# A weight conversion with an empty tick, an earlier second transform, and residual stores from another queue

## The chip, the cores and the metric

The kernel runs on one core of a Trainium2 chip. The metric is the device time of one execution in microseconds (us). The engines are TensorE (PE, with its weight loads as PEld), VectorE (DVE), ScalarE (ACT), GpSimd (POOL) and SyncE (SP), which here only issues DMAs. L624 is line 624 of the kernel before.

## What is computed

Three stages on `x` of 4 x 3136 x 256 (batch, sequence, channels), all in float32: a filter in the frequency domain, then two blocks with a hidden width of 1024.

```python
# stage 1: filter along the sequence
X = np.fft.rfft(x, axis=1)
x = np.fft.irfft(X * (filt_r + 1j * filt_i)[None], n=3136, axis=1)
# stage 2 ("a"): token mixing of rank 32, then w1, relu, w2
u = x + (x.transpose(0, 2, 1) @ U @ V).transpose(0, 2, 1)
x = u + np.maximum(u @ w_ch1, 0.0) @ w_ch2
# stage 3 ("b"): layer norm without offset, times g, then w1b, relu, w2b
xn = (x - mean(x)) / sqrt(var(x) + 1e-6) * g_ln
out = x + np.maximum(xn @ w_ch1b, 0.0) @ w_ch2b
```

## The kernel before

**Numbers.** Every product is made from halves: a matrix is split into a rounded high part and a rest (`ah` and `al`, `hh` and `hl`, `w1h` and `w1l`), and three matmuls stand for one. The weights and the filter's companions arrive as 64-bit words and are converted on the chip.

**The steps.** The 12544 tokens are cut into 25 blocks of up to 512 tokens. Each block has an "a" phase (w1 at L624, w2 at L643 to L645) and a "b" phase (w1b at L624, w2b at L651 to L653). A phase has eight steps, one for each 128 of the hidden width. In a step, `m1` makes one hidden tile: six L624 matmuls into `psh`, relu by ACT into `hh` (L627), the rest by DVE into `hl` (L628). `m2`, two steps behind, multiplies it into `pso`. The phases follow each other as a0 a1 a2 b0 b1 a3 b2 a4 b3 and so on, 400 steps in all. The order of each engine is the order in which the program writes its instructions, and the loop over the steps writes it: first `m1`, then perhaps one tick of the transform, then what `todo` holds for the step, then `m2` and, at a phase's end, `end`, then perhaps a unit, and last a tick or so of the weight conversion.

**Phase ends.** At the end of an "a" phase DVE adds the sums to the input into `x2` (L666), a tile with one buffer, so that L666 of the next "a" phase waits until the last one is stored. Then `todo` spreads over the next steps: adding `al` (L672, names `x`), splitting by ACT and DVE, transposing in place (L675, four and five steps behind), the store of the block to `xd` in DRAM as four DMAs (L702, with the second transpose), its load back in the other layout as `x2t` (L708, at the ninth step, one DMA of 512 KB), and the layer norm's statistics. A "b" phase's end writes the result into `x2t` (L686) and stores it by four DMAs (L694). In the kernel before, all of these stores and loads stand on SP's queue, in program order.

**Units.** A unit makes 448 tokens of the input of stage 2: it loads `ic` (L581) and `wt` (L587, the filtered spectrum from `bd` in DRAM), and for each half of the channels it runs four or more small matmuls and one for the token mixing into `psu` (L595, L597), from which ACT and DVE take `ah` and `al` (L170). `psu` lies in the pool `ps_m`, which has two buffers. Unit 7 is the first of the second batch.

**The transform of batches 1 to 3.** It runs beside the steps, a tick at a time. The generator `rest` yields 36 times for each batch: a load, 15 ticks of the first half, a second load, an empty tick, 17 ticks of the second half (split, product with the filter on POOL at L227, spectrum back through PE, `be` by ACT, then stored to `bd`), and a finish, which makes the units of that batch possible. A credit of RATE a step, from step FFT0 on, decides in which steps a tick runs; once batch 1 is finished the rate is 0.4.

**Weight conversion.** 18 jobs turn the 64-bit words into halves. A job's pieces are: absolute value and low word by ACT, four integer operations by DVE (`words`, L746 to L749), a product and a sum by POOL (L763, L764, into `ct`), then `keep` and `last`. For w1 and w2, `keep` is ACT's copy into the high part and `last` POOL's or DVE's subtraction (L842). For w1b, `keep` is DVE's product with g (`wg`, L832), and behind every second job a `center` takes off the column means: two matmuls with a matrix of 1/256 into `psw` (L848, again in pool `ps_m`), DVE's subtraction (L852), ACT's copies and POOL's rests (L854). Each tick moves every live job on by one piece. `brisk` is set once the first units are made; from then on there is one tick a step, for steps 0 to 23 or so. POOL also issues the loads of these weights, with a DMA of its own queue for each job (L740, `stg`).

The lines of the loop that set where a tick of the transform stands:

```python
if idx > FFT0:
    credit += RATE if 1 not in tstk else 0.4
    if credit >= 1:
        credit -= 1
        next(rest, None)
```

Of the kernel before, what the change touches and what calls it, by code (L numbers as in the profile page):

```python
# [20 lines left out]
P = 128  # L21
# [22 lines left out]
PARTS, UPARTS = (0, 1, 2, 5, 6, 8), 10  # L44
CALLS = (0, 0, 0, 1) + tuple(range(1, 24))
LEAD = 3
FFT0, RATE = 26, 0.75

XTURN, XREAD, XSTAT, XROOT = (3, 4), 8, (10, 11), 12
BW = 32  # L50
# [88 lines left out]
def fft_mixer_kernel(ctx: ExitStack, tc: tile.TileContext, x, U, V, flt, w1, w2, gln, w1b, w2b,  # L139
                     c_fwd32, c_d32, c_e32, c_fwd, c_inv, c_e, c_d, c_w, out):  # L140
    nc = tc.nc
# [43 lines left out]
    xd = [dram.tile([BLK, D], F32, name=f"xd{k}") for k in range(NBLK)]  # L185
# [388 lines left out]
    def blen(k):  # L574
        return min(BLK, NTOK - k * BLK)
# [79 lines left out]
    def end(ph):  # L655
# [3 lines left out]
        if kind == "a":  # L659
            x2 = mp.tile([P, BLK // BW, BW, KT], F32, tag="x2", name="x2", bufs=1)  # L660

            def cut(t, dh):
                return t[k][:, dh, :n].rearrange("p (j c) -> p j c", c=BW)

            for dh in range(KT):
                nc.vector.tensor_tensor(out=x2[:, :n // BW, :, dh], in0=acc[dh][:, :n].rearrange("p (j c) -> p j c", c=BW),  # L666
                                        in1=f32(cut(acth, dh)), op=ALU.add)
            while len(todo) <= XROOT:
                todo.append([])
            for dh in range(KT):  # L670
                o, ah, al = x2[:, :n // BW, :, dh], cut(acth, dh), cut(actl, dh)
                todo[dh].append(lambda o=o, al=al: nc.vector.tensor_tensor(out=o, in0=o, in1=f32(al), op=ALU.add))  # L672
                todo[dh + 1].append(lambda o=o, ah=ah: acopy(ah, o))
                todo[dh + 2].append(lambda o=o, ah=ah, al=al: sub(al, o, f32(ah)))
                todo[XTURN[dh]].append(lambda o=o: nc.vector.transpose(out=o, in_=o))  # L675
            todo[XTURN[-1]].append(lambda: x2store(k, x2))
            todo[XREAD].append(lambda: x2load(k))
            for j, at in enumerate(XSTAT):
                todo[at].append(lambda j=j: x2stat(k, j))
            todo[XROOT].append(lambda: x2root(k))  # L680
            return
# [16 lines left out]
    def x2store(k, x2):  # L698

        n = blen(k)  # L700
        for i in range(P // BW):
            nc.sync.dma_start(xd[k].rearrange("(j t) (i c) -> t j i c", t=BW, i=P // BW)[:, :n // BW, i],  # L702
                              x2[i * BW:(i + 1) * BW, :n // BW].rearrange("p j c k -> p j (c k)"))

    def x2load(k):
# [37 lines left out]
    def words(s, h, t):  # L743

        hb, tb = h.bitcast(I32), t.bitcast(I32)
        nc.vector.tensor_scalar(out=h, in0=h, scalar1=TOP, scalar2=None, op0=ALU.min)  # L746
        nc.vector.tensor_scalar(out=tb, in0=hb, scalar1=3, scalar2=None, op0=ALU.logical_shift_left)
        nc.vector.scalar_tensor_tensor(out=tb, in0=s[:, :, 1], scalar=-0x80000000, in1=tb, op0=ALU.bitwise_and, op1=ALU.bitwise_or)
        nc.vector.tensor_scalar(out=hb, in0=tb, scalar1=-0x800000, scalar2=None, op0=ALU.bitwise_and)  # L749

    def to32(i, s, keep, last):


        p, n = s.shape[:2]
        tags = ("xs", "ya") if brisk and i % 2 else ("yh", "yl")
        h, lf = (fp.tile([P, 512], F32, tag=tag, name=f"c{tag}", bufs=3 if tag == "ya" else 2)[:p, :n] for tag in tags)
        nc.scalar.activation(out=h, in_=s[:, :, 1].bitcast(F32), func=AF.Abs, scale=2.0 ** -112)
        nc.scalar.activation(out=lf, in_=s[:, :, 0].bitcast(U32), func=AF.Copy, scale=2.0 ** -52)
        yield
        t = fp.tile([P, 2 * (D + R)], F32, tag=("fhi", "flo")[i % 2], name="ct", bufs=2)[:p, :n]  # L760
        words(s, h, t)
        yield
        nc.gpsimd.tensor_tensor(out=lf, in0=lf, in1=h, op=ALU.mult)  # L763
        nc.gpsimd.tensor_tensor(out=t, in0=t, in1=lf, op=ALU.add)  # L764
        yield
        keep(t)
        yield
        last(t)
        yield

    after = []
    aside, brisk = nc.vector, False

    def stagger(jobs):

        words, live, fetched = {}, [], 0
        after.clear()

        def fetch(n):
            nonlocal fetched  # L780
            while fetched < min(n, len(jobs)):
                words[fetched] = jobs[fetched][0]()
                fetched += 1

        def advance():
            nonlocal live
            while after:
                after.pop()()
            live = [g for g in live if next(g, 0) is None]

        for n in range(4):
            fetch(n + 1)
            yield
        for i in range(len(jobs) + 4):
            if brisk:
                advance()
            if i < len(jobs):
                live.append(to32(i, words.pop(i), *jobs[i][1:]))
                next(live[-1])
            yield  # L800
            advance()
            if brisk:
                fetch(i + 3)
            yield
            if not brisk:
                advance()
                fetch(i + 3)
                yield
# [73 lines left out]
    with tc.manual_schedule():  # L882
# [6 lines left out]
        def chain():  # L889
            for b in range(1, NB):  # L890
                yield from fft(b)

        first = First()
        pr = stagger([w_job("w1", w1, 0, "wt"), w_job("w1", w1, 1, "wt"), v_job(0), v_job(1)] + [w_job(nm, w, j) for nm, w, j in (
            ("w2", w2, 0), ("w1", w1, 2), ("w1", w1, 3), ("w2", w2, 1), ("w2", w2, 2),
            ("w2", w2, 3), ("w1b", w1b, 0), ("w1b", w1b, 1), ("w2b", w2b, 0), ("w1b", w1b, 2), ("w1b", w1b, 3),
# [64 lines left out]
        brisk = True  # L961
# [61 lines left out]
```

## Time and profile before

| | |
|---|---|
| median of 3 runs | 1402.79 us |
| the runs | 1405.51, 1402.31, 1402.79 us |
| the profiled execution's own time | 1402.46 us |
| its span in the trace | 1400.7 us |
| PE busy | 1358.4 us, 97% |
| DVE busy | 802.0 us, 57% |
| ACT busy | 549.8 us, 39% |
| POOL busy | 173.9 us, 12% |
| moved by DMA | 152.29 MB, mean 109 GB/s |

The page of the profile gives for each engine how long it was busy. An engine close to the whole span sets the time; for such an engine the few microseconds in which it stood still are read one by one: when they were, and which instruction of which engine ended them. The granted clock (PEclk) says how fast PE was allowed to run in a stretch, as a share of full speed. Busy time at half clock is longer, so it is not idle time and doesn't show as such. Times in the timelines count from the start of the span.

### The profile page before, as it was taken

How to read it: one execution, taken by the hardware profiler on the slowest of the kernel's cores; microseconds unless marked ns; L12 is line 12 of the kernel's file. 1: busy time of each engine (PE TensorE's matmuls, PEld its weight loads, DVE VectorE, ACT ScalarE, POOL GpSimd, SP SyncE). 2: the span in 40 equal slices, each digit the busy share in tenths (PEclk: the TensorE clock that was granted, in tenths of full speed). 3: DMA queues.
4: the chain of work that ended last, by engine and by line, in shares of the span. 5: the costliest groups of instructions: out<-in, count | busy, mean ns of one | idle time of the engine just before them, and what ended most of it. 6: DMA issues, size and time to landing. Idle time of an engine off the chain costs nothing.

```text
span 1400.7 us, 20122 instructions
## 1 busy us (share of the span) xinstructions
PE 1358.4 (97%) x7678; PEld 1173.4 (84%) x7678; DVE 802.0 (57%) x1533; ACT 549.8 (39%) x1048; POOL 173.9 (12%) x170
## 2 busy tenths in 40 slices
PE   8888899999899999999999999999999999999998
PEld 8576789887788888888888887888888888888898
DVE  4777974478554455667554445766444444444444
ACT  4864434366433334445333334544322222222222
POOL 3737511022100001111000001111000000000000
PEclk9899999999999999999999999999999999999999
DMA  9735237555526424444345344353122013201111
GB/s 282 246 77 162 75 82 196 166 163 166 158 56 159 125 89 129 120 142 130 74 118 152 91 131 131 98 168 84 58 65 65 16 49 84 65 16 31 46 46 38
DMA packets 140576, 152.29 MB, mean 109 GB/s; under 512 B 61472, under 2 KB 117696, under 8 KB 140384
## 3 DMA queue, kind: packets, MB, share of 16 engines
q1 hardware_dynamic: 131840, 132.37, 33.4%
q0 software_dynamic: 7776, 17.44, 5.1%
q8 instruction: 60, 0.98, 0.3%
q10 hardware_dynamic: 864, 1.20, 0.2%
q14 instruction: 36, 0.29, 0.1%
HBM read 103.44 MB, written 47.54 MB: 108 GB/s over the span
## 4 chain that ended last, share of the span: by engine, by line
PE 82%; DVE 4%; ACT 2%; DMA 1%; issue 1%; SPq 0%; POOL 0%; DVEq 0%; ACTq 0%; POOLq 0%
PE psh L624 36%; PE pso L653 6%; PE pso L652 6%; PE pso L651 6%; PE pso L643 6%; PE pso L644 5%; PE pso L645 5%; PE psu L595 3%; PE ps L199 2%; PE ps L201 2%; PE ps L200 2%; DVE ya L234 1%; PE psu L597 1%; ACT xs L167 1%; PE pt L255 1%
## 5 line engine op out<-in xcount | busy, mean ns | idle before, releaser
L628 DVE SCALAR_TENSOR_TENSOR hl<-psh,hh 128x512 fp32r<-128x512 f32 (+1 forms) x400 | 271.0, 679 | 427.1 <-ACT hh L627 426.7
L627 ACT ACTIVATE hh<-psh 128x512 fp32r<-128x512 f32 (+1 forms) x400 | 234.9, 588 | 604.5 <-PE psh L624 603.8
L624 PE MATMUL psh<-ah,wb 128*128 128x512 f32 (+1 forms) x800 | 276.7, 387 | 0.2 <-DVE hl L628 0.2
L651 PE MATMUL pso<-wb,hh 128*128 128x256 f32 x784 | 221.1, 282 | 1.1 <-DVE x L666 1.1
L653 PE MATMUL pso<-wb,hl 128*128 128x256 f32 x784 | 221.8, 283 | 0.0
L652 PE MATMUL pso<-wb,hh 128*128 128x256 f32 x784 | 221.7, 283 | 0.0
L624 PEld LDWEIGHTS psh<-ah,wb 128*128 128x128 f32 x800 | 150.3, 189 | 28.0 <-DVE hl L628 0.8
L624 PE MATMUL psh<-ah,w1h 128*128 128x512 f32 (+1 forms) x400 | 157.6, 394 | 5.4 <-DVE hl L628 5.4
L643 PE MATMUL pso<-hh,w2h 128*128 128x512 f32 (+1 forms) x400 | 155.0, 388 | 6.8 <-DVE x2t L686 3.5
L651 PEld LDWEIGHTS pso<-wb,hh 128*128 128x128 f32 x784 | 149.7, 191 | 7.5 <-DVE x L666 1.3
L624 PE MATMUL psh<-al,w1h 128*128 128x512 f32 (+1 forms) x400 | 155.8, 390 | 0.0
L624 PE MATMUL psh<-al,wb 128*128 128x512 f32 (+1 forms) x400 | 155.5, 389 | 0.0
L624 PE MATMUL psh<-ah,w1l 128*128 128x512 f32 (+1 forms) x400 | 155.1, 388 | 0.0
L644 PE MATMUL pso<-hl,w2h 128*128 128x512 f32 (+1 forms) x400 | 154.5, 386 | 0.0
L652 PEld LDWEIGHTS pso<-wb,hh 128*128 128x128 f32 x784 | 149.7, 191 | 5.5
L645 PE MATMUL pso<-hh,w2l 128*128 128x512 f32 (+1 forms) x400 | 154.2, 386 | 0.0
L653 PEld LDWEIGHTS pso<-wb,hl 128*128 128x128 f32 x784 | 149.8, 191 | 0.0
L227 POOL TENSOR_TENSOR xs<-xs,ft 128x512 f32<-128x512 f32 x42 | 55.1, 1312 | 391.4 <-ACT xs L167 383.8
L643 PEld LDWEIGHTS pso<-hh,w2h 128*128 128x128 f32 x400 | 75.4, 188 | 22.5 <-DVE x2t L686 4.4
L624 PEld LDWEIGHTS psh<-ah,w1h 128*128 128x128 f32 x400 | 75.9, 190 | 20.0 <-DVE hl L628 7.5
L624 PEld LDWEIGHTS psh<-ah,w1l 128*128 128x128 f32 x400 | 75.6, 189 | 16.0
L645 PEld LDWEIGHTS pso<-hh,w2l 128*128 128x128 f32 x400 | 75.2, 188 | 15.4
(170 smaller groups left out, 1932.2 us busy)
## 6 DMA issues: line engine op xcount, KB each, us to landing
ft<-flt SPq DMA_DIRECT2D x42, 512.0 KB, 4.4
xd<-x SPq DMA_DIRECT2D x96, 128.0 KB, 2.8
x2t<-xd SPq DMA_DIRECT2D x24, 512.0 KB, 4.5
wt<-bd SPq DMA_DIRECT2D x24, 448.0 KB, 5.8
out<-x2t SPq DMA_DIRECT2D x84, 128.0 KB, 2.1
xt<-x SPq DMA_DIRECT2D x42, 224.0 KB, 3.7
zd<-ze SPq DMA_DIRECT2D x42, 224.0 KB, 2.8
zt<-zd SPq DMA_DIRECT2D x42, 224.0 KB, 3.2
```

The lines of the kernel that those rows point to most:

```text
L199: nc.tensor.matmul(o, lh, rh, start=True, stop=False)
L227: (cross or nc.gpsimd).tensor_tensor(out=xs, in0=xs, in1=ft[:, :, 1], op=ALU.mult)
L595: nc.tensor.matmul(ps[:, m:UN:UW], t[:, m, dh * P:(dh + 1) * P], ic[:, m, :], start=m == 0, stop=False, skip_group_check=True)
L624: nc.tensor.matmul(ps[:, :n], w[:, kt, fs], a[:, kt, :n], start=j == 0, stop=j == 3 * KT - 1)
L627: nc.scalar.activation(out=hh[:, :n], in_=ps[:, :n], func=AF.Relu)
L628: nc.vector.scalar_tensor_tensor(out=hl[:, :n], in0=ps[:, :n], scalar=0.0, in1=f32(hh[:, :n]), op0=ALU.max, op1=ALU.subtract)
L643: nc.tensor.matmul(o, wh[:, f, ds], hh[:, :n], start=f == 0, stop=False)
L644: nc.tensor.matmul(o, wh[:, f, ds], hl[:, :n], start=False, stop=False)
L645: nc.tensor.matmul(o, wl[:, f, ds], hh[:, :n], start=False, stop=f == FT - 1)
L651: nc.tensor.matmul(o, hh[:, cs], wh[:, f, :], start=f == 0 and c % 2 == 0, stop=False, skip_group_check=True)
L652: nc.tensor.matmul(o, hh[:, cs], wl[:, f, :], start=False, stop=False, skip_group_check=True)
L653: nc.tensor.matmul(o, hl[:, cs], wh[:, f, :], start=False, stop=f == FT - 1, skip_group_check=True)
```

## The change

Three things are changed. A job of the weight conversion passes an empty tick between POOL's sum and `keep`, so that the engine that takes the sum does so one step later than before; the jobs' loop is one tick longer. FFT0 and RATE become 22 and 0.72 (26 and 0.75 before). The four stores of a residual block (L702) are issued by POOL and no longer by SP. By the two added lines, line numbers from L765 on are two higher in the changed kernel (L832 is L834 there, L842 is L844, L848 is L850, L852 is L854, L854 is L856).

```diff
-FFT0, RATE = 26, 0.75
+FFT0, RATE = 22, 0.72
...
         for i in range(P // BW):
-            nc.sync.dma_start(xd[k].rearrange("(j t) (i c) -> t j i c", t=BW, i=P // BW)[:, :n // BW, i],
+            nc.gpsimd.dma_start(xd[k].rearrange("(j t) (i c) -> t j i c", t=BW, i=P // BW)[:, :n // BW, i],
                               x2[i * BW:(i + 1) * BW, :n // BW].rearrange("p j c k -> p j (c k)"))
...
         nc.gpsimd.tensor_tensor(out=t, in0=t, in1=lf, op=ALU.add)
         yield
+        if brisk:
+            yield
         keep(t)
         yield
         last(t)
...
-        for i in range(len(jobs) + 4):
+        for i in range(len(jobs) + 5):
```

What this does to the engines' order shows at three places. On PE, the first center (`psw`, behind two jobs of w1b) and the unit that follows it in the kernel before, with the names as above:

```order
L645 MATMUL pso<-hh,w2l 128x512
L848 MATMUL psw<-wg,ones 128x512 x2
L624 MATMUL psh<-ah,w1h 128x512
L624 MATMUL psh<-al,w1h 128x512
L624 MATMUL psh<-ah,w1l 128x512
```

and the same place in the changed kernel, from the end of a step on:

```order
L645 MATMUL pso<-hh,w2l 128x512
L595 MATMUL psu<-ic,wt 112x128 x4
L597 MATMUL psu<-v_sb,tk 128x448
L595 MATMUL psu<-ic,wt 112x128 x4
L597 MATMUL psu<-v_sb,tk 128x448
L850 MATMUL psw<-wg,ones 128x512 x2
L624 MATMUL psh<-ah,w1h 128x512
```

Before, the center stands between two steps, and the unit stands one whole step (six L624 rows and the six of w2) further on; now the center stands directly behind the unit.

On DVE, the integer operations of a job (L746 to L749, with the names `cxs`, `cyh`) around the first two products with g (`wg`), before:

```order
L566 COPY wt_1270<-psw 112x512
L832 TENSOR_SCALAR wg<-ct,g_sb 128x512
L746 TENSOR_SCALAR cxs<-cxs 128x512
L747 TENSOR_SCALAR ct<-cxs 128x512
L748 SCALAR_TENSOR_TENSOR ct<-stg,ct 128x512
L749 TENSOR_SCALAR cxs<-ct 128x512
L628 SCALAR_TENSOR_TENSOR hl<-psh,hh 128x512 x2
L832 TENSOR_SCALAR wg<-ct,g_sb 128x512
```

and in the changed kernel:

```order
L566 COPY wt_1269<-psw 112x512
L746 TENSOR_SCALAR cxs<-cxs 128x512
L747 TENSOR_SCALAR ct<-cxs 128x512
L748 SCALAR_TENSOR_TENSOR ct<-stg,ct 128x512
L749 TENSOR_SCALAR cxs<-ct 128x512
L628 SCALAR_TENSOR_TENSOR hl<-psh,hh 128x512
L834 TENSOR_SCALAR wg<-ct,g_sb 128x512
L628 SCALAR_TENSOR_TENSOR hl<-psh,hh 128x512
```

The product with g has moved behind the integer operations of the next job and behind one `hl`.

On SP, at the end of the "b" phase ahead of the second batch's first unit (`out` is the result's store, `x2t` the load of a residual block, `ic` and `wt` a unit's loads), before:

```order
L694 DMA out<-x2t_3093 32x4x256 x4
L708 DMA x2t_3814<-xd4_97 128x4x256
L581 DMA ic_3836<-c_inv 112x448
L587 DMA wt_3835<-bd1_119 112x1024
L581 DMA ic_3862<-c_inv 112x448
L587 DMA wt_3861<-bd1_119 112x1024
```

and in the changed kernel:

```order
L694 DMA out<-x2t_3127 32x4x256 x4
L581 DMA ic_3815<-c_inv 112x448
L587 DMA wt_3814<-bd1_119 112x1024
L286 DMA xt_3818<-x 112x512
L286 DMA xt_3820<-x 112x512
L708 DMA x2t_3824<-xd4_97 128x4x256
L581 DMA ic_3868<-c_inv 112x448
```

The first unit's two loads now stand ahead of the load of the residual block, and the first two loads of the next batch's transform (`xt`) between them.

## Rows read from the trace of the kernel before

**Rows 1.** Page, busy time: engine, us, share of span, instructions.

```profile
PE 1358.4 (97%) x7678; PEld 1173.4 (84%) x7678; DVE 802.0 (57%) x1533; ACT 549.8 (39%) x1048; POOL 173.9 (12%) x170
```

**Rows 2.** Stretches: length, PE PEld DVE ACT POOL busy, PEclk, DMA share, GB/s.

```profile
125.00:157.00 32.00, 27.88 (x118) 21.60 (x118) 25.69 (x41) 14.00 (x26) 20.54 (x19) 0.95 0.40 120
157.00:184.00 27.00, 24.91 (x105) 19.25 (x104) 25.32 (x41) 12.58 (x20) 14.98 (x13) 1.00 0.36 93
184.00:296.00 112.00, 112.00 (x686) 100.05 (x685) 62.76 (x128) 46.10 (x88) 9.33 (x15) 1.00 0.56 152
...
376.00:388.00 12.00, 7.53 (x36) 6.50 (x35) 2.74 (x5) 2.64 (x6) 0.00 (x0) 0.86 0.90 242
...
384.60:388.00 3.40, 3.40 (x17) 3.31 (x17) 0.62 (x1) 0.54 (x1) 0.00 (x0) 0.50 0.93 225
```

**Rows 3.** Waits of PE, 98 to 184 us: us in sum, times, longest.

```profile
PE psh L624 <- DVE hl L628: 4.6, 5, 2.0
PE pso L643 <- DVE x L666: 3.2, 2, 1.7
```

**Rows 4.** Timeline of DVE: start, us, instruction, in brackets idle before and releaser.

```profile
133.55 0.49 DVE L832 TENSOR_SCALAR wg<-ct,g_sb 128x512 f32<-128x512 f32 x1 [2.19 <-POOL ct L764]
...
134.41 0.55 DVE L747 TENSOR_SCALAR ct<-cyh 128x512 int32<-128x512 int32 x1
```

**Rows 5.** Timeline of PE in the conversions: behind the unit, and two waits.

```profile
144.88 0.40 PE L624 MATMUL psh<-ah,w1h 128*128 128x512 f32 x1
...
152.53 0.80 PE L624 MATMUL psh<-ah,w1h 128*128 128x512 f32 x1 [2.01 <-DVE hl L628]
...
170.79 0.50 PE L643 MATMUL pso<-hh,w2h 128*128 128x512 f32 x1 [1.71 <-DVE x L666]
```

**Rows 6.** Timeline of DVE from the first block's transpose to the second's `x`.

```profile
158.73 0.70 DVE L675 STREAM_TRANSPOSE x<-x 128x512 f32<-128x512 f32 x1
...
164.30 1.28 DVE L852 TENSOR_TENSOR wg<-wg,psw 128x512 f32<-128x512 f32 x2 [1.24 <-PE psw L848]
...
165.96 1.40 DVE L747 TENSOR_SCALAR ct<-cyh 128x512 int32<-128x512 int32 x1
...
170.05 1.28 DVE L666 TENSOR_TENSOR x<-pso,ah 128x512 f32<-128x512 f32 x2
```

**Rows 7.** Timeline of DVE, the unit's subtraction behind the first center.

```profile
149.04 0.69 DVE L170 TENSOR_TENSOR al<-psu,ah 128x256 fp32r<-128x256 f32 x2 [0.45 <-ACT ah L167]
```

**Rows 8.** Timelines of SP's queue and of PE, unit 7.

```profile
376.61 0.54 SPq L708 DMA_DIRECT2D x2t<-xd  x1
...
377.83 0.38 SPq L587 DMA_DIRECT2D wt<-bd  x1
...
384.12 1.17 PE L595 MATMUL psu<-ic,wt 112*128 112x112 f32 x6 [4.47 <-DMA wt<-bd]
```

**Rows 9.** Line 587 from 370 to 390 us, two loads.

```profile
DMA to landing us min/median/max: 6.2/7.0/7.7
```

**Rows 10.** Waits of PE, 285 to 376 us, and one row of its timeline.

```profile
PE ps L199 <- ACT be L167: 3.3, 8, 1.0
...
600.61 0.36 PE L595 MATMUL psu<-ic,wt 112*128 112x112 f32 x1 [0.96 <-ACT be L167]
```

**Rows 11.** Line 702 from 150 to 200 us, eight stores.

```profile
DMA to landing us min/median/max: 2.2/2.8/3.0
```

**Rows 12.** POOL's DMA issues: timeline (one) and groups by line (busy, mean ns).

```profile
134.15 0.56 POOL L957 DMA_DIRECT2D d_sb<-c_d  x1
...
L740 POOL DMA_DIRECT2D stg<-w2b x4 | 3.0, 762 | 11.8 <-issue 6.1 <-ACT hh L627 2.6 <-ACT wt L167 2.3
...
L740 POOL DMA_DIRECT2D stg<-w1b x4 | 2.3, 574 | 7.3 <-DVE cxs L749 2.6 <-ACT ah L167 1.6 <-ACT w2h L167 1.6
```

**Rows 13.** Timeline of DVE, second block's transpose to third block's `x`.

```profile
187.23 0.71 DVE L675 STREAM_TRANSPOSE x<-x 128x512 f32<-128x512 f32 x1
...
192.55 0.69 DVE L666 TENSOR_TENSOR x<-pso,ah 128x512 f32<-128x512 f32 x1 [0.72 <-DMA xd<-x]
```

## The prediction

> **What bounds the kernel now.** I read the page first. TensorE (PE) is busy 1358.4 us of a span of 1400.7 us, 97% [rows 1]. The change removes no matmul, so all it can win is PE's idle time, about 42 us in the whole run, and the stretches in which PE ran at a lower clock. Next I cut the span into stretches [rows 2]. In the last two thirds of the weight conversions (125 to 184 us) PE is idle for 32.00 − 27.88 = 4.12 us and 27.00 − 24.91 = 2.09 us, and the granted clock is 0.95 in the first of these two; from 184 to 296 us PE is never idle; the twelve microseconds around the second batch's first unit have 4.5 us of idle time at a clock of 0.86. DVE is the busy neighbour in the conversions: 25.69 us of 32 and 25.32 us of 27, so a wait that goes there meets an engine with almost no room.
>
> Then the waits. Between 98 and 184 us PE waits for DVE, five times for `hl` (4.6 us) and twice for the residual `x` (3.2 us) [rows 3]. I read DVE's own order to see what makes it late [rows 4]: twice it waits for POOL's sum `ct` before it can write `wg` (2.19 us at 133.55 us; the row at 127.69 us is of the same kind, with 2.09 us), and the second such wait stands some 3 us ahead of the first block's `x`. So the first edit aims at a place where PE does lose time.
>
> **The empty tick.** Before, the piece whose sum POOL was given in one tick is taken by ACT or DVE in the next; now one tick later. Removed from DVE: 2.09 + 2.19 us of waits for POOL. The center of `w1b`'s second half moves a step, so DVE's 1.24 us wait for `psw` and the 1.28 us of work behind it [rows 6] stand after `x` at 170.05 us and no longer ahead of it; PE's 1.71 us wait at that place [rows 5] should shrink. Added: the first center's two matmuls now stand behind the unit and not 2.7 us ahead of it. They take a buffer of the unit's own pool, which DVE's `al` of the unit's first half must free. DVE is behind there: it ends that subtraction (its second piece, the first of two from 149.04 us) at about 149.4 us [rows 7], while PE came out of the unit at 144.88 us [rows 5]. So PE waits up to 4.5 us, and 0.2 us if DVE keeps all of the 4.28 us won ahead of it; I take the middle, 2.4 us. Behind the waiting `psw` stands the next step's whole L624 row. Behind each center, `hl` waits for `hh`, which on ACT stands behind two copies of the centered weights and two absolute values. PE's 2.01 us wait at 152.53 us [rows 5], right behind the first center, is of this kind, and the change leaves its cause. PE's waits before 125 us stay as they are, since nothing on DVE waits for POOL in steps 3 to 6. So of the 4.12 + 2.09 = 6.2 us idle, 2.0 us stay and 2.4 us come new: 1.8 us gained, less half of a slow stretch (0.8 us, half of the 1.7 us priced below) that a wait of 2.4 us may bring: −1.0 us. The bounds: everything goes, with the clock, which at 0.95 over 32 us cost 1.6 us, 7.8 us; I use 6.5 us, since one wait of the new kind must stay. On the other side 4.5 us are added at the center and next to nothing goes: +4. Nearest row for my value: DVE's busy 25.3 to 25.7 us per stretch, which the tick does not lower.
>
> **The transform from step 22 on.** The first tick moves from step 28 to 24, the last from 74 to 73. The first unit of batch 1 stays behind step 75. What changes is SP's order. Before, its `wt` load stood behind the 512 KB load of `x2t` and was issued at 377.83 us, landing 6.2 us later at 384.03 us; PE had been ready at 384.12 − 4.47 = 379.65 us [rows 8, 9]. Now `ic` and `wt` stand right behind the four stores of `out`, so `wt` goes out one issue earlier, at 377.83 − 0.6 = 377.2 us, without the 512 KB ahead of it; at the 242 GB/s of that stretch [rows 2] these took 2.2 us. Landing: 377.2 + 6.2 − 2.2 = 381.2 us, wait 1.6 us in place of 4.47: −2.9 us. The clock: from 384.6 to 388 us PE ran at 0.50 [rows 2], which cost 1.7 us. A wait of 2.01 us was followed by such a stretch (152.53 us, clock 0.95 over the 32 us), one of 1.71 us was not (170.79 us, clock 1.00) [rows 2, 5]; so at 1.6 us I count it as gone: −1.7 us. Sum −4.6 us; bounds −0.6 us (only the earlier issue counts) and −6.2 us (all of it).
>
> The ticks of the second half spread a little: 22 steps before, 23 now. Its eight waits of PE for ACT's `be` sum to 3.3 us [rows 10]; scaled by 0.72/0.75 and with fewer runs of three in a row, about −0.7 us. But a unit's turn at step 59 now meets such a tick, and where a unit met one in the later trace PE waited 0.96 us (600.61 us) [rows 10]. Together +0.3 us. Batches 2 and 3 keep their grid of 0.4 a step, one tick further along: their stalls stay.
>
> **The stores on POOL's queue.** Each residual block is stored by four DMAs of 32 x 16 pieces of 256 bytes. From SP they land at most 3.0 us after their issue [rows 11]. No POOL-issued DMA of 512 pieces is in the trace. POOL takes 574 ns to issue one of 128 pieces (`w1b`) and 762 ns for one of 256 (`w2b`) [rows 12]; the line through both gives 574 + 3 × 188 = 1138 ns for 512, an estimate. Bounds: 574 ns, the cheaper row (no price per piece), and 2 × 762 = 1524 ns. So four take 2.3 to 6.1 us, by the line 4.6 us, and 7.6 us until the last has landed.
>
> Who waits for that? `x2` has one buffer, so the next block's `x` (L666) waits for the store. In steady state 11 steps of some 2.8 us (170.05 to 192.55 us is eight steps) lie between, and the load L708 stands four steps behind: both hidden. But a0, a1 and a2 follow each other, and there it is three steps, 8.2 us. For a0 the store can begin when the transpose ends, 158.73 + 0.70 = 159.4 us; `x` stood at 170.05 us [rows 6], and at 170.05 − 1.24 − 1.28 = 167.5 us once it is ahead of the center: 8.1 us against 7.6. I take 0. For a1: 187.23 + 0.71 = 187.94 us, `x` at 192.55 us after a wait of 0.72 us for this very store, 4.6 us in all [rows 13]. With 5.3 to 9.1 us in place of 4.6, `x` comes 0.7 to 4.5 us later, by the line 3.0 us. PE was never idle there [rows 2], so it has some slack; half is my value, +1.5 us, bounds 0 and +4. On POOL itself the fetch of `w2b`'s last piece is queued behind a0's stores: 4.6 us later, covered by two steps' room. The store of block 3 stands ahead of L227's filter product of the transform, which ACT and then PE wait for behind it: one more wait of the eight's mean, 3.3 / 8 = 0.4 us. SP loses 96 issues, but no wait of PE is for an SP issue behind a store, so that gains nothing.
>
> What speaks for a dearer store is a rule, weighed here by itself. The trace has a POOL-issued DMA beside DVE's L747: 0.56 us at 134.15 us [rows 4, 12], no longer than the 574 ns of the `w1b` fetches. The Trainium skill, "SBUF — State Buffer", section "SBUF: two separate sides", holds that DVE in a two-port mode locks POOL out of writing descriptors, and that such a DMA of some 620 ns took some 3100 ns; by that the store of a0 and a1 would be far dearer, and the third rival below would be the likeliest. The row does not bear it out for one DMA of few pieces; no run here shows it for 512.
>
> **Sum.** −1.0 − 4.6 + 0.3 + 1.5 + 0.4 = −3.4 us against the profiled execution's 1402.46 us (span 1400.7 us and 1.8 us around it): 1399.06 us. The median, 1402.79 us, is 0.33 us above that execution, so 1399.4 us.
>
> **Rivals.** First: the tick does all that it can, −6.5 us in place of −1.0, and the store of a1 hides: 1399.4 − 5.5 − 1.5 = 1392.4 us. For it: DVE's two waits and the center's were 5.5 us in sum, ahead of PE's waits. Against it: DVE's load and the center behind the unit. Second: the `wt` load doesn't do what I say, since the DMA queues are busy with `out` and `xt` anyway and PE's wait stays over 2 us with its slow clock: 1399.4 + 4.0 = 1403.4 us. For it: the DMA share of 0.90 in that stretch [rows 2]. Third, slower: a store costs POOL 1.8 us or more. Then a0's four take 7.2 + 3.0 = 10.2 us against 8.1, PE waits 2.1 us, and a1's `x` is 5.6 us late, some 4 us on PE; both waits are over 2 us and each brings a slow stretch of 1.7 us: +9.5 us in place of my +1.5, 1407.4 us and up. For it: DVE and POOL stretch each other, L747 took 1.40 us beside POOL's subtraction at 165.96 us [rows 6] and 0.55 us beside its DMA at 134.41 us [rows 4]. Against it: POOL's DMA rows vary little.
>
> **How the numbers follow.** The measurement can tell a change from none at about 0.3%, 4.2 us: faster is below 1398.6, slower above 1407.0 us. My forecast has 0.53; its time is just inside "same", so 0.24 of that lies below 1398.6 and 0.29 within; first rival 0.20, all faster; second 0.15, all same; third 0.12, all slower. Faster 0.44, same 0.44, slower 0.12. The range must reach into the first rival and to the foot of the third: 1391.5 to 1407.0 us.
>
> **What would show it.** In the changed trace: DVE's waits for POOL's `ct` at L834 gone; a PE wait at `psw` behind the unit of the first center; PE's wait for `wt` near 385 us below 2 us and no clock of 0.50 behind it; four L702 rows on POOL near 1.1 us each; `x` at step 25 some 3 us later with a wait for the store. Wrong it would be if the stores cost over 1.8 us each, if PE's idle time between the conversions' second third and their end fell below 2.5 us or rose above 10, or if `wt` still landed after 383 us.

## The result and the profile after

The changed kernel takes 1414.8 us, the median of four runs (1412.2 to 1416.12), against 1402.81 us before: a ratio of 1.0079, 95% interval 1.0059 to 1.0100. It is slower by 11 us (8 to 14), where 1399.4 us and a range from 1391.5 to 1407.0 us had been forecast. The profiled execution of the changed kernel is its fastest one, 1412.2 us with a span of 1410.4 us, 9.7 us longer than the span before; what the traces show below adds up to those 9.7 us.

Where they are shows if the start of each of the 400 steps (its first L624 matmul) is compared between the two traces. The offset after minus before, in us, at the beginning of some steps:

| step | 0 | 10 | 14 | 22 | 49 | 75 | 76 | 399 |
|---|---|---|---|---|---|---|---|---|
| after − before | 0.6 | 0.7 | 4.2 | 7.4 | 7.5 | 11.5 | 10.7 | 9.4 |

Steps 10 to 22 (the conversions) lose 6.8 us, the second half of the transform (49 to 75) loses 4.0 us, the first unit of the second batch (75 to 76) wins 0.8 us, and the rest wins 1.3 us. The head of the program, ahead of step 0, is the same code in all kernels of this study and lasts from 98.1 to 101.5 us in their profiled executions, shortest in the kernel before. So the traces are compared from step to step, and the times by their medians.

The stretches of the changed kernel, columns as in [rows 2]:

```profile
125.00:157.00 32.00, 27.93 (x117) 21.20 (x116) 24.92 (x35) 13.90 (x26) 20.70 (x18) 0.89 0.42 123
157.00:184.00 27.00, 22.02 (x88) 15.75 (x86) 23.78 (x34) 9.60 (x17) 15.41 (x15) 1.00 0.41 103
...
394.80:398.20 3.40, 3.40 (x16) 3.36 (x17) 0.49 (x1) 0.54 (x1) 0.00 (x0) 0.52 1.08 275
```

Against [rows 2]: the idle time of the first is the same, 4.1 us, but its granted clock fell from 0.95 to 0.89; the second has 5.0 us of idle time where there were 2.1. The third is the first unit of the second batch, which still runs at half the clock.

The waits of PE in the changed kernel from 98 to 190 us (us in sum, times, longest), to be held against [rows 3]:

```profile
PE psh L624 <- DVE hl L628: 7.0, 6, 2.2
PE psw L850 <- DVE al L170: 3.2, 1, 3.2
PE psu L595 <- ACT wt L167: 1.0, 1, 1.0
PE pso L643 <- DVE x L666: 0.9, 1, 0.9
PE pso L645 <- POOL w2l L844: 0.6, 1, 0.6
```

The wait for `x` shrank from 3.2 to 0.9 us, as the empty tick meant it to. The waits for `hl` grew from 4.6 to 7.0 us, and a new one stands at `psw`, the center behind the unit. By steps: gone are the 2.0 us at step 14 (for `hl`) and the 1.7 us at step 18 (for `x`); new are 3.2 us at step 11 (`psw`) and 0.8, 1.2, 1.6 and 2.2 us at steps 15, 16, 20 and 21 (`hl`).

DVE's own waits in the same stretch, first before, then after:

```profile
DVE wg L832 <- POOL ct L764: 4.3, 2, 2.2
...
DVE hl L628 <- ACT hh L627: 2.9, 4, 1.1
DVE wg L852 <- PE psw L848: 1.2, 1, 1.2
```

```profile
DVE hl L628 <- ACT hh L627: 9.0, 6, 2.8
...
DVE wg L854 <- PE psw L850: 2.8, 1, 2.8
```

This is the heart of the result. DVE's 4.3 us of waiting for POOL are gone. In their place it waits 6.1 us longer for ACT's `hh` and 1.6 us longer for PE's `psw`. Why ACT is late shows in its timeline behind the first center of the changed kernel:

```profile
151.02 1.23 ACT L167 ACTIVATE wb<-wg 128x512 fp32r<-128x512 f32 x2 [3.98 <-DVE wg L854]
152.15 0.62 ACT L167 ACTIVATE wb<-ct 128x512 fp32r<-128x512 f32 x1
152.67 0.65 ACT L757 ACTIVATE cyh<-stg 128x512 f32<-128x512 f32 x1
153.23 0.65 ACT L758 ACTIVATE cyl<-stg 128x512 f32<-128x512 uint32 x1
153.78 0.58 ACT L627 ACTIVATE hh<-psh 128x512 fp32r<-128x512 f32 x1
```

The two copies of the centered weights wait for DVE; behind them stand the next job's copy and the absolute values of the job after it, and only then `hh`. Before the change the center lay in a step that had the copies but no absolute values. The same stands behind the second center, with the same 2.8 us.

The two absolute values are 1.1 of these 2.8 us. The rest shows because DVE has nothing left to do there. In the kernel before it had the next job's four integer operations between the center's subtractions and `hl`, and `hl` did not wait (behind the second center, L852 at 164.30 us in [rows 6]):

```profile
165.51 0.42 DVE L746 TENSOR_SCALAR cyh<-cyh 128x512 f32<-128x512 f32 x1
...
169.45 0.68 DVE L628 SCALAR_TENSOR_TENSOR hl<-psh,hh 128x512 fp32r<-128x512 f32 x1
```

In the changed kernel DVE stands idle there, and the integer operations follow one step later, behind a job's last subtraction (L844; L746 starts at 157.73 us):

```profile
150.30 1.28 DVE L854 TENSOR_TENSOR wg<-wg,psw 128x512 f32<-128x512 f32 x2 [2.80 <-PE psw L850]
154.39 0.69 DVE L628 SCALAR_TENSOR_TENSOR hl<-psh,hh 128x512 fp32r<-128x512 f32 x1 [2.81 <-ACT hh L627]
...
156.01 1.79 DVE L844 TENSOR_TENSOR wb<-ct,wb 128x512 fp32r<-128x512 f32 x1
```

And the center itself, on PE:

```profile
146.51 3.75 PE L850 MATMUL psw<-wg,ones 128*128 128x512 f32 x4 [3.17 <-DVE al L170]
...
150.48 0.63 PE L624 MATMUL psh<-al,w1h 128*128 128x512 f32 x1
```

The 3.17 us are the wait for a buffer of the unit's pool. L624, 0.39 us otherwise, takes 0.63 us behind it: from 148 to 158 us the granted clock is 0.77 in the changed kernel.

### The profile page after: what moved, and what is told of

The parts are those of the page before. It is cut to its first block, busy times and chain, and to the rows that moved or that the text cites. A ratio compares the mean times of both kernels' runs of the same rounds, so it can differ in the third digit from the quotient of the medians.

```text
span 1410.4 us, 20171 instructions
## 1 busy us (share of the span) xinstructions
PE 1358.9 (96%) x7678; PEld 1170.9 (83%) x7678; DVE 810.0 (57%) x1533; ACT 549.5 (39%) x1048; POOL 239.2 (17%) x270
## 4 chain that ended last, share of the span: by engine, by line
PE 84%; DVE 8%; ACT 3%; DMA 2%; issue 2%; POOL 1%; SPq 0%; DVEq 0%; ACTq 0%; POOLq 0%
PE psh L624 35%; PE pso L653 6%; PE pso L651 6%; PE pso L652 6%; PE pso L643 5%; PE pso L644 5%; PE pso L645 5%; PE psu L595 3%; PE ps L199 2%; PE ps L200 2%; PE ps L201 2%; DVE hl L628 1%; PE pz L423 1%; ACT xs L167 1%; DVE ya L234 1%
## 5 line engine op out<-in xcount | busy, mean ns | idle before, releaser
L624 PE MATMUL psh<-ah,wb 128*128 128x512 f32 (+1 forms) x800 | 276.7, 387 | 0.5 <-DVE hl L628 0.5
L624 PEld LDWEIGHTS psh<-ah,wb 128*128 128x128 f32 x800 | 150.3, 189 | 28.0 <-DVE hl L628 0.7
L624 PE MATMUL psh<-ah,w1h 128*128 128x512 f32 (+1 forms) x400 | 158.2, 395 | 8.0 <-DVE hl L628 7.9
L624 PE MATMUL psh<-al,w1h 128*128 128x512 f32 (+1 forms) x400 | 155.7, 389 | 0.0
L624 PE MATMUL psh<-al,wb 128*128 128x512 f32 (+1 forms) x400 | 155.5, 389 | 0.0
L624 PE MATMUL psh<-ah,w1l 128*128 128x512 f32 (+1 forms) x400 | 154.8, 387 | 0.0
L702 POOL DMA_DIRECT2D xd<-x x100 | 64.6, 654 | 520.6 <-DVE x L675 519.9
L624 PEld LDWEIGHTS psh<-ah,w1h 128*128 128x128 f32 x400 | 75.8, 189 | 24.2 <-DVE hl L628 11.6
L624 PEld LDWEIGHTS psh<-ah,w1l 128*128 128x128 f32 x400 | 75.5, 189 | 15.9
```

What stands on the lines that cost most here:

```text
L624: nc.tensor.matmul(ps[:, :n], w[:, kt, fs], a[:, kt, :n], start=j == 0, stop=j == 3 * KT - 1)
L702: nc.gpsimd.dma_start(xd[k].rearrange("(j t) (i c) -> t j i c", t=BW, i=P // BW)[:, :n // BW, i], x2[i * BW:(i + 1) * BW, :n // BW].rearra ...
```

## The experiments

All times below are medians; "before" was run beside each and had 1403.2 to 1403.7 us there. Differences to before are worked out from the ratio, times 1403 us. T is the empty tick, F the transform's new start and rate, Q the stores on POOL's queue.

### The three parts, each alone

**t_only** adds only the two edits of the tick to the kernel before:

```diff
+        if brisk:
+            yield
...
-        for i in range(len(jobs) + 4):
+        for i in range(len(jobs) + 5):
```

> Only the empty tick is added to the kernel before. Theory A (the first center now stands behind the unit, waits there for DVE to free its PSUM buffer, and a stretch of lower clock follows): most of the loss is here, 1402.8 + 6 to 8 = 1409 to 1411 us, with PE waiting about 3 us at the first psw (L850) and a granted clock near 0.77 in the ten microseconds behind it. Rival B (the stores on POOL's queue hold up POOL's sums and the centered weights): the tick alone costs nothing or gains 1 us, 1401.5 to 1403 us, and the wait at psw is below 1 us.

Measured: 1408.78 us against 1403.58, ratio 1.0044 (1.0029 to 1.0059), some 6.2 us slower, just below theory A's band. Its two signs are there: a wait of 3.19 us at the first `psw`, and a granted clock of 0.75 from 148 to 158 us. PE's waits from 98 to 190 us sum to 12.5 us, where they were 8.5.

**f_only** changes one line of the kernel before:

```diff
-FFT0, RATE = 26, 0.75
+FFT0, RATE = 22, 0.72
```

> Only FFT0 and RATE are changed. Theory A: the second half of the second transform loses about 4 us by its new neighbours (a wait for x2t, one for yh, a unit beside a tick), the first unit's load gains about 1 us: 1405 to 1407 us. Rival B (the transform is not at fault, those waits come from POOL's filter product behind the stores): 1398 to 1402 us, with PE's waits in that half at 3.5 us or less.

Measured: 1410.34 us, ratio 1.0053 (1.0034 to 1.0073), 7.4 us slower; more than theory A said. The waits of PE from 98 to 400 us hold what was known from the changed kernel and one more:

```profile
PE psu L595 <- DMA wt<-bd: 3.3, 1, 3.3
PE pso L651 <- DVE x L666: 2.4, 1, 2.4
PE ps L199 <- ACT be L167: 2.2, 6, 0.7
PE pso L643 <- DVE x2t L686: 1.5, 1, 1.5
PE psu L595 <- ACT be L167: 1.0, 1, 1.0
PE ps L199 <- ACT yh L167: 0.9, 1, 0.9
```

The 2.4 us are at step 26. SP's queue and the timelines of ACT and DVE tell why:

```profile
188.24 2.17 SPq L702 DMA_DIRECT2D xd<-x  x4
190.46 1.82 SPq L286 DMA_DIRECT2D xt<-x  x3
...
194.53 0.63 ACT L167 ACTIVATE hi<-xt 112x512 fp32r<-112x512 f32 x1 [3.11 <-DMA xt<-x]
...
195.19 0.69 DVE L170 TENSOR_TENSOR lo<-xt,hi 112x512 fp32r<-112x512 f32 x1 [3.05 <-ACT hi L167]
195.80 1.28 DVE L666 TENSOR_TENSOR x<-pso,ah 128x512 f32<-128x512 f32 x2
```

The transform's first loads `xt` stand on SP behind the second block's stores, which wait for DVE's transpose. They land late, ACT waits for them, DVE waits for ACT, and `x` (L666) of the third block stands behind that on DVE. A granted clock of 0.55 from 196.5 to 200 us follows, so that steps 22 to 27 lose 3.0 us.

**q_only** changes the queue of the stores alone:

```diff
-            nc.sync.dma_start(xd[k].rearrange("(j t) (i c) -> t j i c", t=BW, i=P // BW)[:, :n // BW, i],
+            nc.gpsimd.dma_start(xd[k].rearrange("(j t) (i c) -> t j i c", t=BW, i=P // BW)[:, :n // BW, i],
```

> Only the four stores of a residual block are issued by POOL. Theory A: near nothing, 1402.5 to 1405 us, the stores at 0.65 us each on POOL. Rival B: 5 us or more, 1408 us and up, with PE's idle time from 157 to 376 us grown by 4 us.

Measured: 1405.89 us, ratio 1.0022 (1.0011 to 1.0033), 3.1 us slower. The time lies 0.9 us above theory A's band and 2.1 us below rival B's. The line of the stores, from 150 to 220 us:

```profile
L702 POOL DMA_DIRECT2D xd<-x x12: 651/652/762, 163.0 to 215.7; - x12
...
DMA to landing us min/median/max: 2.7/3.1/4.5
```

A store of 512 pieces costs POOL 0.65 us, and lands up to 4.5 us after its issue (3.1 us in the median), where SP's landed within 3.0 us (2.8 us) [rows 11]. `x` at step 26 now waits 2.0 us for the store on DVE (0.72 us before, [rows 13]), and PE 0.7 us for `x`.

**fq** has F and Q without T.

> The transform from step 22 at 0.72 and the stores on POOL, without the empty tick. Theory A (part of the early transform's loss is that on SP's queue its first loads xt stand behind the second block's stores, which wait for DVE's transpose, so DVE waits for xt ahead of x at step 26): with the stores on POOL that wait goes, the two parts cost less than their sum, 1402.8 + 7.4 + 3.1 - 4 = 1409 us. Rival (the parts add up): 1413 us.

Measured: 1408.27 us, ratio 1.0030 (1.0019 to 1.0042), 4.2 us slower, as theory A said, and no slower than F alone. In its trace no wait of PE is left at step 26: with the stores on POOL the loads `xt` have no store ahead of them on SP, and go out from 166.5 us on, not 190.5 us as in f_only. So F and Q share a loss: steps 22 to 27 lose 3.0 us in f_only, 1.0 us in q_only, nothing in fq and 0.1 us in the changed kernel. This is a part of why the three parts alone (6.2 + 7.4 + 3.1 = 16.7 us) sum to more than the whole change (11 us); the rest is not located, and the intervals are wide (F alone: 4.8 to 10.2 us).

### Why the tick costs

**after_psw** puts the center's sums into another pool, in the changed kernel, and **t_psw** does the same with T alone:

```diff
-            ps = ps_m.tile([P, 512], F32, tag="m", name="psw")
+            ps = ps_t.tile([P, 512], F32, tag="t", name="psw")
```

> The changed kernel with one line changed: the center's sums (psw) lie in PSUM's one-buffer pool ps_t in place of the unit's pool ps_m, so that they wait for no buffer that DVE must free. Theory A: PE's wait of 3.2 us at the first psw goes, with the lower clock behind it: 5 to 6 us less than the changed kernel, about 1409 us. Rival (DVE is late anyway and the wait comes back at the next hl): within 1.5 us of the changed kernel, 1413 to 1416 us, a wait of 2 us or more at L624 in its place.

> Only the empty tick, with the center's sums in the one-buffer PSUM pool ps_t. Theory A (the tick's loss is the center's wait behind the unit and the low clock after it): the 3.2 us wait goes and the time comes 4 us below the tick alone, 1404 to 1406 us. Rival (the tick moves the load of DVE and ACT onto worse steps, and the center is only where it shows): within 1.5 us of the tick alone, 1407 to 1410 us.

Measured: 1411.01 us for after_psw, ratio to before 1.0063 (1.0046 to 1.0079), by the ratios 2.2 us and by the medians 3.8 us below the changed kernel; 1407.32 us for t_psw, ratio 1.0029 (1.0019 to 1.0039), 2.1 us and 1.5 us below the tick alone. after_psw lies between its two expectations, t_psw in the band of its rival. The waits of after_psw from 98 to 190 us, and one stretch of it:

```profile
PE psh L624 <- DVE hl L628: 10.3, 8, 2.2
```

```profile
125.00:157.00 32.00, 27.12 (x124) 20.96 (x122) 27.62 (x40) 14.77 (x27) 20.98 (x18) 1.00 0.43 123
```

The wait at `psw` is gone and the same three microseconds come back at `hl`, as the rival had it: 12.8 us of waits in sum, 12.7 in the changed kernel. What is won is the clock, 1.00 in place of 0.89 over 32 us: steps 10 to 22 lose 3.9 us in place of 6.8 (t_psw: 3.4 in place of 6.4). One wait of 3.2 us was followed by the lower clock, two of 1.7 and 2.2 us in its place were not.

**t_pool** gives w2b's last subtraction to POOL, in T alone:

```diff
-                (nc.vector if nm == "w2b" else aside).tensor_tensor(out=lo, in0=cut(t), in1=f32(hi), op=ALU.subtract)
+                aside.tensor_tensor(out=lo, in0=cut(t), in1=f32(hi), op=ALU.subtract)
```

> One empty tick, and the last subtraction of w2b's jobs on POOL in place of DVE. Theory A (one empty tick loses because DVE has this subtraction and the next job's integer operations in one step): the waits for hl at steps 15, 16, 20 and 21 shrink by more than half and the time comes 2 to 4 us below the one empty tick, 1405 to 1407 us; the first center's wait stays. Rival (POOL's operations beside DVE stretch DVE's by as much): no change, 1408 to 1410 us.

Measured: 1409.44 us, ratio 1.0039 (1.0025 to 1.0053): the rival was right. DVE's timeline behind the first center in this kernel:

```profile
156.79 0.69 DVE L628 SCALAR_TENSOR_TENSOR hl<-psh,hh 128x512 fp32r<-128x512 f32 x1 [2.82 <-ACT hh L627]
...
158.39 1.52 DVE L746 TENSOR_SCALAR cyh<-cyh 128x512 f32<-128x512 f32 x1
159.94 1.40 DVE L747 TENSOR_SCALAR ct<-cyh 128x512 int32<-128x512 int32 x1
```

The subtraction is gone from DVE, but L746 and L747, 0.42 us each where POOL has no arithmetic, take 1.5 and 1.4 us beside POOL, which runs without a pause from 154.1 to 161 us. In t_only the subtraction and these two take 1.79 + 0.41 + 0.43 = 2.6 us at this place, here the two alone take 2.9 us: what DVE is spared it pays back in stretched operations.

**t_two** has two empty ticks:

```diff
+        if brisk:
+            yield
+            yield
...
-        for i in range(len(jobs) + 4):
+        for i in range(len(jobs) + 6):
```

> Two empty ticks in place of one, nothing else of the change. With one empty tick DVE's last subtraction of a job falls into the same step as the integer operations of the next job, before the change they took turns; with two they take turns again, the centers stand at steps 12 and 18, one step behind the unit, and DVE still has no wait for POOL. Theory A (the tick costs by this doubling and by the center behind the unit): PE's idle time in steps 10 to 22 falls to 4 us or less, 1401 to 1403.5 us. Rival (any later keep and last hurts, since the jobs only end later): 1407 us or more.

Measured: 1407.76 us, ratio 1.0025 (1.0011 to 1.0038). In steps 10 to 22 it loses 1.5 us where one tick lost 6.4, which is what theory A was after (PE is idle for 5.5 us there, not for 4 or less; 5.3 us before). The integer operations stand between the center's subtractions and `hl` again (152.6 to 157.7 us), and `hl` does not wait. But the time lies in the rival's band, and for a reason of the rival's kind: jobs that end later. A new wait stands at step 5:

```profile
117.67 0.50 PE L645 MATMUL pso<-hh,w2l 128*128 128x512 f32 x1 [3.43 <-POOL w2l L845]
```

The low part of w2's first piece comes two steps later than in the kernel before, and PE needs it sooner; steps 4 to 10 lose 2.9 us. With one tick the same wait is 0.6 us, before there is none.

**t_late** has one tick and moves the center alone by one step, so that it stands neither behind the unit nor beside the next jobs' copies and absolute values:

```diff
-    after = []
+    after, late = [], []
...
+            while late:
+                late.pop()()
             while after:
                 after.pop()()
...
-                    after.append(center)
+                    after.append(lambda: late.append(center))
```

> One empty tick, and each center one step later (steps 12 and 18), where no copy and no absolute value of other jobs stand beside its two copies on ACT, and the unit lies a step back. Theory A (the tick costs by the center's step): DVE's waits for hh from 98 to 190 us fall from 9.0 us to 5 us or less, PE's loss in steps 10 to 22 from 6.4 us to 1.5 us or less, and the time is 1402 to 1405 us. Rival (the later keep and last cost): no better than the one tick with the center's sums in another buffer, 1406.5 us or more.

Measured: 1406.08 us, ratio 1.0019 (1.0010 to 1.0029). DVE's waits for `hh` are 5.1 us in place of 9.0, and steps 10 to 22 lose 2.7 us in place of 6.4. So the center's step is a little over half of the tick's cost; the time is between the two expectations. What is left is mainly one wait:

```profile
158.87 0.50 PE L624 MATMUL psh<-ah,w1h 128*128 128x512 f32 x1 [3.03 <-DVE hl L628]
```

Ahead of that `hl` DVE has, without a pause from 151.1 us on, the center's subtractions, the last subtraction of a job and the four integer operations of the next: the tick put the last two into one step. But of these, L746 and L747 take 1.52 and 1.38 us beside POOL's rests of the center (L858, 153.7 to 156.7 us), 2.1 us more than where POOL has no arithmetic. Whether the doubled step or POOL beside DVE makes this wait, t_late does not separate.

### The transform's place

**f_22_75** and **f_24_75** and **f_25_75** change the one line of f_only to 22, 24 and 25 with the old RATE of 0.75; the batch is finished at steps 70, 72 and 73 (74 before, 73 in the changed kernel).

> FFT0 = 22 with the old RATE of 0.75: the ticks of the second batch stand exactly four steps earlier than before, in the same pattern of three steps out of four, and the batch is finished at step 70, five steps ahead of its first unit. Theory A (0.72 puts ticks beside phase ends and a unit; the early start costs the wait of x at step 26): the second half of the transform loses no more than before (PE's waits near 3.3 us), the 4.5 us wait for wt and its low clock are gone, the 2.4 us wait at step 26 stays: 1398 to 1401 us. Rival (any earlier transform collides as much): 1407 us or more.

> FFT0 = 24 with RATE 0.75: two steps earlier than before, first tick at step 26, finished at step 72. Theory A: nothing of the transform stands ahead of x at step 26, so that wait is gone; the ticks' pattern is shifted by two against the phase ends, so some waits of 1 to 1.5 us for x2t or be come (PE's waits in the second half 4 to 6 us); the wait for wt goes: 1398 to 1402 us. Rival: 1405 us or more.

> FFT0 = 25 with RATE 0.75: one step earlier than before, so the second batch is finished at step 73, where the changed kernel has it too (72 with FFT0 = 24, 74 before). Theory A (what decides the unit's wait is whether the batch is finished ahead of the phase end at step 73, whose four result stores stand ahead of wt on SP): wt still waits 3 to 4 us with the low clock, and the time is 1402 to 1406 us. Rival (one step earlier is enough, and in the changed kernel other things delay wt): the wait is below 1 us, 1397 to 1399 us.

Measured: f_22_75 1400.63 us, ratio 0.9976 (0.9967 to 0.9986); **f_24_75 1397.83 us, ratio 0.9954 (0.9939 to 0.9969)**, which beats both kernels; f_25_75 1405.28 us, ratio 1.0012 (1.0002 to 1.0021). Theory A's bands hold in all three, f_24_75 a little better than its band; but in f_22_75 the wait at step 26 is another one, 1.7 us for ACT's `hi`. Finished at 70 or 72, the unit waits for no `wt`, and the step from 75 to 76 is 6.3 us shorter than before (offsets 2.45 and −3.86 us in f_24_75). Finished at 73, it waits 3.4 us (f_25_75), and the granted clock behind it is 0.59 from 388 to 392 us. The time of f_25_75 alone would not show this, since its second half (steps 49 to 75) loses 5.2 us besides, where f_24_75 loses 1.2 us. SP's queue in f_24_75 shows the difference:

```profile
372.00 0.86 SPq L581 DMA_DIRECT2D ic<-c_inv  x1
375.15 0.30 SPq L587 DMA_DIRECT2D wt<-bd  x1
377.04 2.50 SPq L694 DMA_DIRECT2D out<-x2t  x4
```

The unit's loads stand ahead of the result's stores. In the changed kernel they stand behind them:

```profile
387.03 2.51 SPq L694 DMA_DIRECT2D out<-x2t  x4
389.63 0.54 SPq L581 DMA_DIRECT2D ic<-c_inv  x1
390.27 0.39 SPq L587 DMA_DIRECT2D wt<-bd  x1
...
394.80 1.90 PE L595 MATMUL psu<-ic,wt 112*128 112x112 f32 x8 [3.66 <-DMA wt<-bd]
```

### The stores' queue

**q_act** issues the stores from ACT's queue (`nc.scalar` in the line of q_only).

> Only the queue of the residual's stores: ACT's in place of SP's (POOL's in the change). Theory A (what the stores on POOL cost is the later landing, 6 us from the transpose to the end against 4.6 on SP, where the third block's x waits for it): ACT's queue waits for DVE's transpose ahead of ACT's own work, so PE loses several us by late hh, 1408 us or more. Rival (any queue but SP's is as good): 1403 to 1406 us.

Measured: 1415.09 us, ratio 1.0079 (1.0061 to 1.0097), as theory A said. A queue that is also an engine with work waits for the transpose in place: where ACT issued them at 189.5 us, its next `hh` had waited 3.9 us behind the stores.

```profile
189.51 2.17 ACTq L702 DMA_DIRECT2D xd<-x  x4
191.79 1.08 ACT L627 ACTIVATE hh<-psh 128x512 fp32r<-128x512 f32 x2 [3.93 <-DMA xd<-x]
```

### On top of the better start

**f24_q** is f_24_75 with the stores on POOL, **f24_late** is f_24_75 with t_late's edits.

> FFT0 = 24 and RATE = 0.75 with the residual's stores on POOL's queue. Theory A (the stores on POOL cost by their later landing at steps 18 and 26 and by standing ahead of the filter product): 1 to 3 us above FFT0 = 24 alone, 1399 to 1401 us. Rival (what they cost alone was the wt load's chance): no difference, 1397 to 1398.5 us.

> FFT0 = 24 and RATE = 0.75 with the empty tick and the late center. Theory A: the tick is near neutral there too, 1397 to 1399.5 us, and a gain over FFT0 = 24 alone (1397.8 us) would be 1 us at most. Rival: 1401 us or more.

Measured: f24_q 1401.11 us, ratio 0.9982 (0.9973 to 0.9992), 3.3 us above f_24_75 by the medians and just above theory A's band, so the stores on POOL cost there too; from step 0 on its trace loses 2.4 us against that of f_24_75, 0.9 of them in steps 22 to 27, where PE again waits 0.7 us for `x`. f24_late 1401.38 us, ratio 0.9988 (0.9978 to 0.9998), 3.5 us above it: the rival was right, the tick costs there as well. No form of the tick that was tried wins anything.

## Why the prediction was wrong

Between the −3.4 us that were forecast and the +9.7 us of the traces lie 13.1 us. The tick makes 7.8 of them, the unit's load 3.8 and the second half of the transform 3.7; the rest works the other way.

**The tick: −1.0 us forecast, +6.2 us alone, +6.8 us in the changed kernel's steps 10 to 22.** This is the step that failed, and with it the sign. Right was what it removes (DVE's two waits for POOL), that `x` would come sooner (3.2 to 0.9 us), and that the center would wait behind the unit (2.4 us taken, 3.2 us measured). Two things were wrong. First, I took the removed waits as time won. DVE's waits for POOL were replaced by waits for ACT: I had written that ACT's copies and absolute values stand ahead of `hh` behind each center, and then counted that as a cause that stays, at the 2.0 us of one wait before. That wait (152.53 us in [rows 5], step 14) was not of this kind:

```profile
151.78 0.69 DVE L628 SCALAR_TENSOR_TENSOR hl<-psh,hh 128x512 fp32r<-128x512 f32 x1 [0.58 <-ACT hh L627]
```

The `hl` ahead of it waited only 0.58 us for `hh`. DVE was late because L746, L747, L748 and L672, 2.2 us in sum where POOL has no arithmetic, took 6.0 us beside POOL from 141.3 to 148.3 us, and the unit's `al` stood behind them. In the changed kernel this wait is gone. The kind that I described is new there: behind each center the absolute values are new on ACT, the integer operations that had filled DVE's time are gone, and DVE's waits for `hh` went from 2.9 to 9.0 us. t_late, which moves the center out of that step, wins back 3.7 of the 6.4 us that the tick alone loses in steps 10 to 22. Second, the even and odd steps: the empty tick moved a job's last subtraction into the step of the next job's integer operations, where before they took turns. That this makes the other 2.7 us is read from the order and not shown: t_two, where they take turns again, loses 1.5 us there, but it moves the center too, and in t_late POOL stretches the same operations. The half of a slow stretch that I allowed came whole: the clock over 32 us went from 0.95 to 0.89, 1.9 us.

**The unit's load: −4.6 us forecast, −0.8 us measured.** The order on SP was as read, and `wt` went out one issue earlier on that queue. But the queue itself was later against PE. The four stores of `out` ahead of it wait for DVE's L686, and the transform's finish, now at step 73, stands ahead of that on DVE:

```profile
385.17 0.40 DVE L267 TENSOR_TENSOR tt<-pt,tt 32x256 f32<-32x256 f32 x1
386.07 0.42 DVE L170 TENSOR_TENSOR tk<-tt,tk 32x256 fp32r<-32x256 f32 x1 [0.50 <-ACT tk L167]
386.52 1.66 DVE L686 SCALAR_TENSOR_TENSOR x2t<-pso,ln,x2t 128x256 f32<-128x256 f32 x4
```

Before, `wt` was issued 379.65 − 377.83 = 1.8 us ahead of PE's readiness, now 391.14 − 390.27 = 0.9 us. The landing I had taken as 4.0 us was 4.4 us. The wait of 3.66 us kept the slow stretch (0.52 from 394.8 to 398.2 us). That the mechanism was right, and only its place wrong by one step, f_24_75 and f_25_75 show: the unit's loads must be ahead of the phase's end, then all 6.2 us of my bound are won (6.3 us measured). My second rival named this outcome, but for another reason (busy DMA queues).

That the finish stands at step 73 at all is a matter of rounding. Fifty steps of 0.72 make exactly the 36 ticks, so by the decimal numbers the last tick falls at step 72, as in f_24_75; but the credit is a float and stands at 0.9999999999999987 in step 72 when the loop's lines are run, so the tick waits for step 73. A rate a little above 0.72, which would put it back, was not run.

**The second half of the transform: +0.3 us forecast, +4.0 us measured.** PE's waits there grew from 3.3 to 6.3 us, which is 3.0 of the 4.0 us. The unit's collision at step 59 came as read (0.96 us taken, 1.0 us measured), and the waits for `be` fell by 1.1 us where 0.7 had been forecast. Missed were 1.2 us of waits at step 53 (for `yh` and `yl`), and this:

```profile
318.55 0.50 PE L643 MATMUL pso<-hh,w2h 128*128 128x512 f32 x1 [1.47 <-DVE x2t L686]
```

A tick at step 57, where a phase ends, makes DVE late with L686, and PE needs the sums' buffers in step 58. Before, a tick stood in step 58 as well; its matmuls, I take it, gave DVE the time. In f_only, f_25_75 and the changed kernel there is a tick at 57 and none at 58, and all three show the 1.5 us; f_24_75 has none at 57 and f_22_75 one in each, and neither shows it. Scaling by the rate missed what decides: where a tick stands. The matmul right behind such a wait also takes about 0.1 us longer (0.50 us here, 0.39 us otherwise), which is a part of the last 1.0 us; the rest of it is not located.

**The stores: +1.9 us forecast, 3.1 us (1.5 to 4.6) measured alone.** The issue costs 0.65 us and not 1.14 (the price does not grow in a line with the pieces), and the landing is up to 4.5 us and not 3.0. So `x` at step 26 starts some 6 us behind the transpose in q_only, where I had 7.6 and the kernel before has 4.6. The term was right in kind: steps 22 to 27 lose 1.0 us in q_only's trace (1.5 forecast), and in the changed kernel, where PE is already late, PE waits only 0.2 us. The filter product's 0.4 us came too: steps 49 to 75 lose 0.5 us. Put at nothing was the unit, where `wt` comes later (PE waits 4.9 us, before 4.5) and steps 75 to 76 lose 0.9 us. That the sum is near is in part luck. A dearer store was weighed in that part: POOL's 12 stores in q_only, beside DVE's work, take 0.65 to 0.76 us each. The third rival (1.8 us a store) is out; the changed kernel is slower than 1407 us for another reason than the one it named.

**What stays open.** The changed kernel's other three runs are 1.6 to 3.9 us above its profiled one, and of these there is no trace. Whether the rest of the tick's loss in t_late goes if the last subtraction is moved to another step, or if POOL's rests of the center are, was not tried.

## What to carry to other kernels

A wait that is taken off an engine is won only if nothing else of the same step ends later: before an operation is moved by a step, list for each engine what that step already holds and what the step that it leaves now lacks, and count the neighbour that the next wait would name. Where one loop hands out pieces in turns (even and odd steps), one empty slot changes what meets what, and moves each later consumer, as the 3.4 us for `w2l` with two ticks show. A transfer that is needed at a fixed place is moved ahead of the queue's blocking entry, here the stores that wait for a phase's end; one entry nearer won 0.8 us here, ahead of the entry 6.3 us.

## What the runs showed of the chip

A DMA issued by POOL cost it 0.65 us with 512 pieces, 0.76 us with 256 and 0.57 us with 128 [rows 12], so the number of pieces alone does not set the price. DVE's operations L746 and L747 of 0.42 us took 1.4 to 1.5 us while POOL ran its products and differences beside them. And twice the same idle time cost differently: 12.7 us of waits with one of 3.2 us among them came with a clock of 0.89 over 32 us, 12.8 us in shorter waits with a clock of 1.00, a difference of 2.9 us over steps 10 to 22. One wait does not settle it: the 3.03 us wait of t_late at step 15 was followed by 0.83 from 158 to 168 us, the 3.01 us wait of f24_late at the same step by 1.00 there.
